# Joining float64 words into float32: three passes over 256 columns, or two over 512

## Chip, cores, metric

The kernel runs on one core of a Trainium2 chip. What counts is the device time of one execution in microseconds. The engines are named as the profile does: PE (TensorE), DVE (VectorE), ACT (ScalarE), POOL (GpSimd) and SP (SyncE, which issues most transfers); each works through its own queue in order.

## What is computed

```python
# q, k, v: (8, 8, 576, 64) float32; the five weights arrive as float64
attn = softmax(q @ mean_of_8(k).T / 8) @ mean_of_8(v)        # per head, 72 pooled keys
x = attn.transpose(0, 2, 1, 3).reshape(4608, 512)
h = x @ w_in                                                  # 512 x 2048
x = (h * clip(h + 3, 0, 6) / 6) @ w_out                       # 2048 x 512
g = x @ w_gate                                                # 512 x 1536
out = (g * sigmoid(g) * (x @ w_val)) @ w_out2                 # 1536 x 512
```

## The kernel before

TensorE multiplies in float32 pieces: each operand is kept as a high part and a low part (the rest), and each product is three matmuls, so that every weight and every activation is split once (`split`, lines 136 and 137: a cast on ScalarE gives the high part, a subtraction gives the low part).

The program has three stages. In the startup (to about 56 us) the attention of the first block of 512 tokens is computed. Then come nine token blocks (loop over j) of the first feed-forward part. A block has 16 iterations (f), one for each 128 columns of `w_in`: an up-projection into `h`, its activation (`act1`, lines 575 and 577), the split of the result `g` (`split_g`), and, two iterations later, the down-projection into `y` (`down1`); both products are on line 553. Between these, `attn_slot` puts the attention steps of the next block, in an order written out by hand. From about 1040 us on the second feed-forward part runs, as a Strassen-like scheme on prepared sums of weights.

The weights of the first part are needed from block 0 on, so they are converted during the startup and block 0. A float64 word arrives as two 32-bit words. `fetch` (line 104) loads them into a ring of staging tiles `wstg`, on SyncE's queue; `rescale` (line 115, ScalarE) multiplies the upper word, read as a float32, by 2^-112, which moves the exponent to its float32 place; `join` (VectorE) makes the float32 word in a tile `w` in three passes: line 120 shifts the upper word left by 4 and right by 1, line 126 ors in the lower word shifted right by 29, line 131 ors in the sign bit of the upper word. `split` then writes the parts into `wu` (up) or `fly` (down); the subtraction is on GpSimd. In block 0, and there alone, the split of `g` subtracts on GpSimd too; in the later blocks it does so on VectorE.

`Weights.convert` is one step of that pipeline: it splits what the call before joined, joins what the call before rescaled, rescales what has been fetched, and fetches anew. One call handles two pieces of 256 columns, that is one weight tile of 512 columns. The tiles `w` come from a pool of two buffers (`t_p`, tag w32), so one call uses both. There are 32 tiles, 16 up and 16 down, in the order up 0, up 1, down 0, up 2, down 1 and so on. In the startup some units call it once; in block 0 each iteration calls it twice. A finished down tile also goes to DRAM (`w1_d`), from where the later blocks read it.

The weights of the second part are prepared during blocks 1 to 7, in 18 units (`prep_step`), one every six iterations: four quarters of 256 columns are fetched, rescaled, and joined into the tile `q`; GpSimd forms sums of them, and the parts go to DRAM.

Of the kernel before, what the change touches and what calls it, by code (L numbers as in the profile page):

```python
# [8 lines left out]
F32 = mybir.dt.float32  # L9
# [14 lines left out]
def kernel(  # L24
# [54 lines left out]
    prep_ctx = ExitStack()  # L79
    stg_p = prep_ctx.enter_context(tc.tile_pool(name="stg", bufs=6, side="right"))  # L80
    q7_p = prep_ctx.enter_context(tc.tile_pool(name="q7", bufs=1, side="right"))
# [17 lines left out]
    wu = {}  # L99
    WC = 256  # L100

    def fetch(src):
        t = stg_p.tile([P, WC, 2], F32, tag="stg", name="wstg")
        nc.sync.dma_start(
            out=t.bitcast(I32).rearrange("p a b -> p (a b)") if len(src.shape) == 2
            else t.bitcast(I32).rearrange("p (k a) b -> p k (a b)", k=src.shape[1]),
            in_=src,
        )
        return t

    def rescale(stage):
        hi = stage[:, :, 1]
        nc.scalar.activation(out=hi, in_=hi, func=ACTF.Copy, scale=2.0 ** -112)

    def join(pieces):
        for stage, dst in pieces:
            hi = stage[:, :, 1].bitcast(I32)
            nc.vector.tensor_scalar(  # L120
                out=dst, in0=hi, scalar1=4, scalar2=1,
                op0=ALU.logical_shift_left, op1=ALU.logical_shift_right,
            )
# [15 lines left out]
    class Weights:  # L139


        def __init__(self):
            self.todo, self.staged, self.scaled, self.joined = [], [], [], []
            self.cur = {}

        def add_up(self, key, src, f):
            w = src.bitcast(I32).rearrange("(k p) f -> p k f", p=P)[:, :, 2 * P * f:2 * P * (f + 1)]
            for i in range(KT * P // WC):
                m = WC // P
                self.todo.append(("up", key, w[:, m * i:m * (i + 1)], i))  # L150

        def add_down(self, key, src, f):
            w = src.bitcast(I32)[f * P:(f + 1) * P, :]
            for i in range(DM // WC):
                self.todo.append(("down", key, w[:, 2 * WC * i:2 * WC * (i + 1)], i))

        def fetch(self):
            while self.todo and len(self.staged) + len(self.scaled) < 6:
                item = self.todo.pop(0)
                self.staged.append((item, fetch(item[2])))  # L160

        def convert(self, n=1):

            done, self.joined = self.joined, []
            for (kind, key, _, i), t in done:
                if i == 0:
                    if kind == "up":
                        self.cur[key] = wu_p.tile([P, 2, KT, P], F32R, tag="wu", name="wu")
                    else:
                        self.cur[key] = fly_p.tile([P, 2, DM], F32R, tag="fly", name="fly")  # L170
                w = self.cur[key]
                if kind == "up":
                    w = w.rearrange("p a k f -> p a (k f)")
                w = w[:, :, WC * i:WC * (i + 1)]
                split(w[:, 0], w[:, 1], f32(t), nc.gpsimd)
                if i == KT * P // WC - 1:
                    t = self.cur.pop(key)
                    (wu if kind == "up" else fly)[key] = t
                    if kind == "down":
                        nc.sync.dma_start(out=w1_d[key[1]], in_=f32(t))  # L180
# [42 lines left out]

    PREP = 6
    prep_t = {}

# [7 lines left out]
    def prep_step(u, step):  # L234
        kind, f, m = preps[u]
        if step == 0:
            place = A7 if kind == "up" else B7
            prep_t["q", u] = []
            for quarter in ("11", "12", "21", "22"):
                r, c = int(quarter[0]) - 1, int(quarter[1]) - 1  # L240
                if kind == "up":
                    w = (w_gate, w_val)[m].bitcast(I32).rearrange("(k p) f -> p k f", p=P)
                    src = w[:, 2 * c:2 * c + 2, 2 * P * (2 * f + r):2 * P * (2 * f + r + 1)]
                else:
                    w = w_out2.bitcast(I32)[P * (2 * f + r):P * (2 * f + r + 1), :]
                    src = w[:, 4 * P * c:4 * P * (c + 1)]
                prep_t["q", u].append((fetch(src), place[quarter]))
        elif step == 1:
            for s, _ in prep_t["q", u]:
                rescale(s)  # L250
        elif step == 2:
            q = prep_t["f", u] = q7_p.tile([P, 8, WC], F32, tag="q7", name="q7")
            join([(s, q[:, i].bitcast(I32)) for s, i in prep_t.pop(("q", u))])
        elif step == 3:
# [5 lines left out]
        elif step == 4:  # L260
            q, t = prep_t["f", u], s7_p.tile([P, 7, 2, WC], F32R, tag="s7", name="s7")
            prep_t["s", u] = t
# [643 lines left out]
    def do_step(st):  # L906
# [29 lines left out]
        elif what == "X":  # L936
            exps(units[i])
        elif what == "M":
            scale_e(units[i])
        elif what == "U":  # L940
            copy_a(units[i])
        elif what == "L":
            lo_a(units[i])
        elif what == "W":
            hi_x(units[i])
        elif what == "Y":
            lo_x(units[i])
# [16 lines left out]
    with tc.manual_schedule():  # L964
# [30 lines left out]
        while ("in", 1) not in wu:  # L995
            weights.convert(2)

# [23 lines left out]
        for n, (j, f) in enumerate(seq1):  # L1021
# [13 lines left out]
            g = act1(hp)  # L1035
            weights.convert(2 if j == 0 else 0)
            if n >= 2:
# [5 lines left out]
            split_g((1, j, f), g)  # L1043
            weights.convert(2 if j == 0 else 0)
            if j > 0:
# [76 lines left out]
```

## Time and profile before

| | us |
|---|---|
| median of 3 runs | 1835.23 (1834.75 to 1835.96) |
| the profiled execution | 1835.06 |
| its span, first to last instruction | 1833.3 |
| PE busy in the span | 1748.5 (95%) |
| DVE / ACT / POOL busy | 1258.8 / 686.8 / 676.6 |
| PE share of the chain that ended last | 81% |

Busy times are averages over stages with different limits. What a change in one stage is worth has to be read in that stage. Line numbers (L120) are those of the kernel before.

### The profile page before, as it was taken

The page shows a single profiled execution, that of the slowest core. Times are in us where ns is not written, and L with a number is a line of the kernel's source. Part 1 is how long each engine was busy: PE and PEld are TensorE (multiplying, and loading weights), DVE is VectorE, ACT ScalarE, POOL GpSimd, SP SyncE. Part 2 cuts the span into 40 slices and gives each one's busy share as a digit, 9 for nine tenths or more (in the row PEclk, how much of TensorE's full clock was granted, in tenths as well). Part 3 has the DMA queues.
Part 4 walks back from the last instruction along what each step waited for, and adds up shares of the span by engine and source line. Part 5 has one row for each costly group of instructions (what it writes and reads, how often), then busy time and mean ns, then how long its engine had stood idle before and what let it go on. Part 6 is the DMA issues. An engine that isn't in the chain of part 4 may idle for free.

```text
span 1833.3 us, 28479 instructions
## 1 busy us (share of the span) xinstructions
PE 1748.5 (95%) x9929; PEld 1575.9 (86%) x9929; DVE 1258.8 (69%) x2480; ACT 686.8 (37%) x1612; POOL 676.6 (37%) x833
## 2 busy tenths in 40 slices
PE   4687899999999998999999999999999999999999
PEld 3476688888878787878888899999999999999999
DVE  6787676876767677686542367767678668568666
ACT  5444344443444444444433223224224225124223
POOL 5455342331423325233114154153252352361450
PEclk8888999999999999999999999999999999999999
DMA  7555456665766656656553487887887977977876
GB/s 159 173 174 162 148 172 200 216 185 183 215 206 197 197 168 195 209 159 197 194 177 132 177 294 238 296 288 241 305 277 252 315 262 250 324 252 253 284 245 219
DMA packets 203103, 402.97 MB, mean 220 GB/s; under 512 B 90576, under 2 KB 126416, under 8 KB 192208
## 3 DMA queue, kind: packets, MB, share of 16 engines
q1 hardware_dynamic: 198256, 396.17, 66.9%
q10 hardware_dynamic: 4704, 4.98, 0.9%
q8 instruction: 79, 1.29, 0.3%
q14 instruction: 64, 0.52, 0.1%
HBM read 340.79 MB, written 60.29 MB: 219 GB/s over the span
## 4 chain that ended last, share of the span: by engine, by line
PE 81%; DVE 7%; DMA 5%; issue 2%; POOL 2%; ACT 2%; SPq 1%; ACTq 0%; POOLq 0%; DVEq 0%
PE b L660 43%; PE y L553 17%; PE h L553 16%; PE pss L445 2%; DMA y<-yo 1%; DVE w L126 1%; DVE w L131 1%; DMA vts<-in_v_dram 1%; PE pst L505 1%; DMA qs<-in_q_dram 1%; DVE w L120 1%; PE pst L509 1%; DVE kp L370 1%; DMA fly<-w1d 1%; PE psk L393 1%
## 5 line engine op out<-in xcount | busy, mean ns | idle before, releaser
L660 PE MATMUL b<-xc,wr 128*128 128x384 f32 x3024 | 525.2, 334 | 0.0
L660 PEld LDWEIGHTS b<-xc,wr 128*128 128x128 f32 x3024 | 524.0, 188 | 0.1
L553 PE MATMUL h<-x,wu 128*128 128x512 f32 x1728 | 435.3, 401 | 0.0
L553 PE MATMUL y<-g,fly 128*128 128x512 f32 x1728 | 430.2, 398 | 1.5 <-DMA fly<-w1d 0.8
L669 DVE TENSOR_TENSOR c<-c,b 128x384 f32<-128x384 f32 x504 | 265.2, 552 | 178.5 <-PE b L660 154.7
L553 PEld LDWEIGHTS h<-x,wu 128*128 128x128 f32 x1728 | 322.0, 191 | 65.3 <-DVE x L546 0.6
L553 PEld LDWEIGHTS y<-g,fly 128*128 128x128 f32 x1728 | 318.3, 189 | 66.4 <-ACT yo L594 1.0
L707 POOL TENSOR_TENSOR s<-s,c 128x384 f32<-128x384 f32 x144 | 142.4, 1013 | 400.2 <-ACT s L705 400.2
L660 PE MATMUL b<-wr,gc 128*128 128x256 f32 x2268 | 265.6, 279 | 0.0
L660 PEld LDWEIGHTS b<-wr,gc 128*128 128x128 f32 x2268 | 265.4, 188 | 0.0
L488 POOL TENSOR_TENSOR e<-e,sm 96x288 f32<-96x288 f32 (+3 forms) x85 | 73.5, 865 | 451.9 <-DVE sm L484 336.1
L714 POOL TENSOR_TENSOR gf<-s,c 128x384 f32<-128x384 f32 x144 | 168.2, 1192 | 67.3 <-DVE c L669 66.5
L136 ACT CAST gc<-gf 128x768 fp32r<-128x768 f32 x126 | 105.7, 839 | 186.6 <-POOL gf L714 101.0
L705 ACT ACTIVATE s<-c 128x384 f32<-128x384 f32 x144 | 73.5, 526 | 202.0 <-DVE c L669 200.9
L137 DVE TENSOR_TENSOR gc<-gf,gc 128x768 fp32r<-128x768 f32 x126 | 133.9, 1095 | 15.5 <-ACT gc L136 13.7
L137 DVE TENSOR_TENSOR g<-g,g 128x512 fp32r<-128x512 f32 x128 | 93.0, 727 | 67.1 <-ACT g L136 66.6
L577 DVE SCALAR_TENSOR_TENSOR g<-t,h 128x512 f32<-128x512 f32 x144 | 97.3, 676 | 59.9 <-ACT t L575 53.5
L136 ACT CAST g<-g 128x512 fp32r<-128x512 f32 x144 | 88.6, 615 | 85.5 <-PE y L553 46.0
L575 ACT ACTIVATE t<-h,three 128x512 f32<-128x512 f32 x144 | 98.2, 682 | 37.1 <-PE h L553 36.4
L475 ACT ACTIVATE e<-e 96x288 f32<-96x288 f32 (+3 forms) x85 | 35.3, 415 | 185.2 <-DVE e L472 183.9
L445 PE MATMUL pss<-kbd,qT 128*128 128x144 f32 (+2 forms) x336 | 63.2, 308 | 29.3 <-DVE x L546 26.4
L677 ACT COPY c<-b 128x384 f32<-128x384 f32 x72 | 33.9, 471 | 145.6 <-PE b L660 145.6
(106 smaller groups left out, 1723.0 us busy)
## 6 DMA issues: line engine op xcount, KB each, us to landing
wr<-sup SPq DMA_DIRECT2D x72, 1024.0 KB
fly<-w1d SPq DMA_DIRECT2D x128, 512.0 KB
wr<-sdn SPq DMA_DIRECT2D x84, 768.0 KB
wr<-sup SPq DMA_DIRECT2D x72, 768.0 KB
sup<-s SPq DMA_DIRECT2D x12, 1792.0 KB
wstg<-in_moe_w_out_dram SPq DMA_DIRECT2D x56, 256.0 KB
sdn<-s SPq DMA_DIRECT2D x6, 1792.0 KB
ystg<-y SPq DMA_DIRECT2D x24, 384.0 KB
```

The lines of the kernel that those rows point to most:

```text
L136: nc.scalar.copy(out=hi, in_=src)
L137: lo_engine.tensor_tensor(out=lo, in0=src, in1=f32(hi), op=ALU.subtract)
L445: nc.tensor.matmul(out=ps[:, i], lhsT=qT[:, i * qt:(i + 1) * qt], rhs=kbd_t[p], start=True, stop=True)
L488: nc.gpsimd.tensor_tensor(out=e3, in0=e3, in1=sm.to_broadcast(list(e3.shape)), op=ALU.mult)
L553: nc.tensor.matmul(out=ps, lhsT=w(kt, wh), rhs=x(kt, xh), start=first and n == 0, stop=last and n == 3 * len(kts) - 1,)
L575: nc.scalar.activation(out=t, in_=ps, func=ACTF.Relu, bias=three)
L577: nc.vector.scalar_tensor_tensor(out=g, in0=t, scalar=6.0, in1=ps, op0=ALU.min, op1=ALU.mult)
L660: nc.tensor.matmul(out=ps, lhsT=w(wh), rhs=x(xh), start=first and n == 0, stop=last and n == 2)
L669: add = lambda dst, a, b: nc.vector.tensor_tensor(out=dst, in0=a, in1=b, op=ALU.add)
L705: nc.scalar.activation(out=g[q], in_=c[q], func=ACTF.Sigmoid)
L707: nc.gpsimd.tensor_tensor(out=g[q], in0=g[q], in1=c[q], op=ALU.mult)
L714: nc.gpsimd.tensor_tensor(out=gf[p][:, GP[TURN[q]], f], in0=g[q], in1=c[q], op=ALU.mult)
```

## The change

Conversion pieces become 512 columns wide, and `join` has two passes in place of three.

- `rescale` uses ScalarE's Prelu with a scale of 2^-112 and a slope of 2^32 for negative values. A negative upper word gets an exponent larger by 32 than a positive one, so the bit that becomes the sign after a shift by 3 is set.
- `join` shifts the upper word left by 3, then ors in the lower word shifted right by 29.
- The ring of staging tiles holds three tiles of 512 columns in place of six of 256. `convert` handles one tile per call in place of two pieces; the calls stay where they were.
- In `prep_step` two quarters share one staging tile (two transfers into its halves), and one join writes both quarters of `q`.

```diff
-    stg_p = prep_ctx.enter_context(tc.tile_pool(name="stg", bufs=6, side="right"))
+    stg_p = prep_ctx.enter_context(tc.tile_pool(name="stg", bufs=3, side="right"))
...
-    WC = 256
+    WC = 512
...
-        nc.scalar.activation(out=hi, in_=hi, func=ACTF.Copy, scale=2.0 ** -112)
-
-    def join(pieces):
-        for stage, dst in pieces:
-            hi = stage[:, :, 1].bitcast(I32)
-            nc.vector.tensor_scalar(
-                out=dst, in0=hi, scalar1=4, scalar2=1,
-                op0=ALU.logical_shift_left, op1=ALU.logical_shift_right,
-            )
-        for stage, dst in pieces:
-            lo = stage[:, :, 0].bitcast(I32)
-            nc.vector.scalar_tensor_tensor(
-                out=dst, in0=lo, scalar=29, in1=dst, op0=ALU.logical_shift_right, op1=ALU.bitwise_or
-            )
-        for stage, dst in pieces:
-            hi = stage[:, :, 1].bitcast(I32)
-            nc.vector.scalar_tensor_tensor(
-                out=dst, in0=hi, scalar=-(2 ** 31), in1=dst, op0=ALU.bitwise_and, op1=ALU.bitwise_or
-            )
+        nc.scalar.activation(out=hi, in_=hi, func=ACTF.Prelu, scale=2.0 ** -112, alpha=2.0 ** 32)
+
+    def join(stage, dst, parts=1):
+        hi, lo = (stage[:, :, i].bitcast(I32) for i in (1, 0))
+        if parts > 1:
+            hi, lo = (t.rearrange("p (k n) -> p k n", k=parts) for t in (hi, lo))
+        nc.vector.tensor_scalar(
+            out=dst, in0=hi, scalar1=3, scalar2=None, op0=ALU.logical_shift_left,
+        )
+        nc.vector.scalar_tensor_tensor(
+            out=dst, in0=lo, scalar=29, in1=dst, op0=ALU.logical_shift_right, op1=ALU.bitwise_or
+        )
...
-            for i in range(KT * P // WC):
-                m = WC // P
-                self.todo.append(("up", key, w[:, m * i:m * (i + 1)], i))
+            self.todo.append(("up", key, w))
...
-            while self.todo and len(self.staged) + len(self.scaled) < 6:
+            while self.todo and len(self.staged) + len(self.scaled) < 3:
...
-            pieces = []
             scaled, self.scaled = self.scaled, []
             for item, s in scaled:
                 t = t_p.tile([P, WC], I32, tag="w32", name="w32")
-                pieces.append((s, t))
+                join(s, t)
                 self.joined.append((item, t))
-            join(pieces)
...
-            for quarter in ("11", "12", "21", "22"):
+            for pair in ((("11", "21"), ("12", "22")) if kind == "up" else (("11", "21"), ("22", "12"))):
+                t = stg_p.tile([P, WC, 2], F32, tag="stg", name="wstg")
+                for i, quarter in enumerate(pair):
...
+                    fetch_into(t[:, WH * i:WH * (i + 1)], src)
...
-            join([(s, q[:, i].bitcast(I32)) for s, i in prep_t.pop(("q", u))])
+            for s, at in prep_t.pop(("q", u)):
+                join(s, q[:, at].bitcast(I32), 2)
...
-            weights.convert(2)
+            weights.convert()
```

## Rows read from the trace of the kernel before

**Rows 1.** The page of the profile: span, and busy tenths of TensorE and VectorE and the granted TensorE clock in 40 equal slices of 45.8 us.

```profile
span 1833.3 us, 28479 instructions
...
PE   4687899999999998999999999999999999999999
...
DVE  6787676876767677686542367767678668568666
...
PEclk8888999999999999999999999999999999999999
```

**Rows 2.** The view by windows: start and end of a stretch in us, its length, busy us (and count) of PE, PEld, DVE, ACT and POOL, granted clock, DMA share, GB/s.

```profile
34.00:206.00 172.00, 125.97 (x590) 99.29 (x589) 135.36 (x339) 80.38 (x254) 91.33 (x130) 0.84 0.52 162
232.00:335.00 103.00, 102.71 (x520) 85.50 (x520) 77.88 (x185) 46.03 (x123) 33.27 (x54) 1.00 0.60 185
232.00:1040.00 808.00, 793.34 (x3858) 655.96 (x3858) 533.71 (x1189) 335.28 (x828) 248.04 (x360) 1.00 0.60 187
```

**Rows 3.** TensorE's timeline (start us, us, what): the first and the fourteenth up-projection of block 0, and a key pooling that ran without a stop; then, from the view of one source line, the first and last start of the 18 stores of finished blocks on ScalarE (line 594, two in each of 9 blocks).

```profile
56.41 5.37 PE L553 MATMUL h<-x,wu 128*128 128x512 f32 x12
...
121.67 2.02 PE L393 MATMUL psk<-ident,k_in 72*64 72x72 f32 x32
...
206.72 2.93 PE L553 MATMUL h<-x,wu 128*128 128x512 f32 x12
...
L594 ACT ACTIVATE yo<-y x18: 590/597/600, 222.7 to 1039.9; 128x512 f32<-128x512 f32 x18
```

**Rows 4.** The chain of waits between 34 and 206 us, shares by line (the view ends the line where it does), and what TensorE waited for longest in the same stretch (us in total, times, longest us).

```profile
by line: issue 14.3%; DVE w L126 10.3%; DVE w L131 8.6%; PE y L553 7.6%; PE h L553 7.0%; DVE w L120 6.3%; PE psk L393 5.4%; DMA wstg<-in_moe_w_in_dram 4.7%; POOL fly L137 4.2%; POOL wu L137 3.4%; PE pss L445 1.7%; ACT wu L136 1.7%; DVE x L5
...
PE pss L445 <- DVE x L546: 20.6, 6, 4.7
```

**Rows 5.** The view by windows for the instructions alone that write or read the tiles named w (the joined 32-bit words): busy us of DVE, ACT and POOL (and counts), then as in rows 2.

```profile
34.00:206.00 172.00, 89.62 (x192) 22.68 (x62) 44.75 (x62) 0.84 0.52 162
```

**Rows 6.** VectorE's groups between 34 and 206 us, by form: the shift of the conversion (busy us, mean ns | idle us of the engine before it, and what ended that).

```profile
L120 DVE TENSOR_SCALAR w<-wstg 128x256 int32<-128x256 int32 x64 | 35.1, 588 | 30.8 <-POOL wu L137 21.1 <-POOL fly L137 6.7 <-DMA q_in<-in_q_dram 2.8
```

**Rows 7.** The timeline (start us, us, engine, what): a conversion call that GpSimd did not disturb, and one pair that it did.

```profile
185.76 2.09 DVE L131 SCALAR_TENSOR_TENSOR w<-wstg,w 128x256 int32<-128x256 int32 x2
185.97 1.25 POOL L137 TENSOR_TENSOR g<-g,g 128x512 fp32r<-128x512 f32 x1
...
193.04 0.49 DVE L120 TENSOR_SCALAR w<-wstg 128x256 int32<-128x256 int32 x2
193.45 0.75 DVE L126 SCALAR_TENSOR_TENSOR w<-wstg,w 128x256 int32<-128x256 int32 x2
194.12 0.75 DVE L131 SCALAR_TENSOR_TENSOR w<-wstg,w 128x256 int32<-128x256 int32 x2
```

**Rows 8.** The view of source line 120: minimum, median and maximum ns, first and last start, in the later preparations (q) and in the conversion (w).

```profile
L120 DVE TENSOR_SCALAR q<-wstg x72: 279/285/836, 247.8 to 922.3; 128x256 int32<-128x256 int32 x72
L120 DVE TENSOR_SCALAR w<-wstg x64: 279/797/1371, 34.3 to 203.2; 128x256 int32<-128x256 int32 x64
```

**Rows 9.** SyncE's queue from 30 to 222 us: what the weight fetches (line 104) waited for longest (us in total, times, longest us); then two fetches in the timeline, and their landing as a piece of the chain of waits.

```profile
SPq L104 <- DVE w L131: 67.4, 28, 7.4
...
127.10 0.89 SPq L104 DMA_DIRECT2D wstg<-in_moe_w_in_dram  x2
...
127.58 2.75 DMA wstg<-in_moe_w_in_dram
```

**Rows 10.** VectorE's and GpSimd's groups between 34 and 206 us, by form: the product of the activation over 512 columns, and the subtractions of the conversion and of g.

```profile
L577 DVE SCALAR_TENSOR_TENSOR g<-t,h 128x512 f32<-128x512 f32 x14 | 9.4, 670 | 1.5 <-ACT t L575 1.4
...
L137 POOL TENSOR_TENSOR wu<-w,wu 128x256 fp32r<-128x256 f32 x32 | 23.2, 744 | 4.7 <-ACT wu L136 4.7
L137 POOL TENSOR_TENSOR fly<-w,fly 128x256 fp32r<-128x256 f32 x30 | 21.6, 740 | 13.3 <-ACT fly L136 13.3
L137 POOL TENSOR_TENSOR g<-g,g 128x512 fp32r<-128x512 f32 x14 | 18.9, 1353 | 2.3 <-ACT g L136 2.3
```

**Rows 11.** ScalarE's groups between 34 and 206 us, by form: the rescaling, a cast of the conversion and the cast of g.

```profile
L115 ACT ACTIVATE wstg<-wstg 128x256 f32<-128x256 f32 x61 | 23.3, 431 | 0.0
L136 ACT CAST fly<-w 128x256 fp32r<-128x256 f32 x30 | 10.8, 402 | 18.6 <-DVE w L131 6.6 <-issue 6.2 <-PE y L553 3.6
...
L136 ACT CAST g<-g 128x512 fp32r<-128x512 f32 x14 | 8.6, 614 | 0.1
```

**Rows 12.** The groups of the whole program by form: the table loads of ScalarE.

```profile
L968 ACT ACT_TABLE_LOAD x1 | 1.3, 1283 | 0.8 <-PEq L1107 0.8
L1051 ACT ACT_TABLE_LOAD x1 | 1.3, 1283 | 0.0
```

**Rows 13.** VectorE's timeline in block 1: the twelve operations of one later preparation.

```profile
247.78 0.89 DVE L120 TENSOR_SCALAR q<-wstg 128x256 int32<-128x256 int32 x4
248.59 1.42 DVE L126 SCALAR_TENSOR_TENSOR q<-wstg,q 128x256 int32<-128x256 int32 x4
249.93 1.42 DVE L131 SCALAR_TENSOR_TENSOR q<-wstg,q 128x256 int32<-128x256 int32 x4
```

More of the change, by code (lines that the diff above doesn't have):

```diff
@@ L99, with fetch_into @@
     wu = {}
-    WC = 256
+    WC = 512
     def fetch(src):
         t = stg_p.tile([P, WC, 2], F32, tag="stg", name="wstg")
+        fetch_into(t, src)
+        return t
+    def fetch_into(t, src):
         nc.sync.dma_start(
@@ L108, in fetch @@
         )
-        return t
     def rescale(stage):
         hi = stage[:, :, 1]
-        nc.scalar.activation(out=hi, in_=hi, func=ACTF.Copy, scale=2.0 ** -112)
-    def join(pieces):
-        for stage, dst in pieces:
-            hi = stage[:, :, 1].bitcast(I32)
-            nc.vector.tensor_scalar(
-                out=dst, in0=hi, scalar1=4, scalar2=1,
-                op0=ALU.logical_shift_left, op1=ALU.logical_shift_right,
-            )
-        for stage, dst in pieces:
-            lo = stage[:, :, 0].bitcast(I32)
-            nc.vector.scalar_tensor_tensor(
-                out=dst, in0=lo, scalar=29, in1=dst, op0=ALU.logical_shift_right, op1=ALU.bitwise_or
-            )
-        for stage, dst in pieces:
-            hi = stage[:, :, 1].bitcast(I32)
-            nc.vector.scalar_tensor_tensor(
-                out=dst, in0=hi, scalar=-(2 ** 31), in1=dst, op0=ALU.bitwise_and, op1=ALU.bitwise_or
-            )
+        nc.scalar.activation(out=hi, in_=hi, func=ACTF.Prelu, scale=2.0 ** -112, alpha=2.0 ** 32)
[9 more added lines that the diff above has]
+        )
     def split(hi, lo, src, lo_engine):
@@ L143, in __init__ @@
             self.todo, self.staged, self.scaled, self.joined = [], [], [], []
-            self.cur = {}
         def add_up(self, key, src, f):
             w = src.bitcast(I32).rearrange("(k p) f -> p k f", p=P)[:, :, 2 * P * f:2 * P * (f + 1)]
-            for i in range(KT * P // WC):
-                m = WC // P
-                self.todo.append(("up", key, w[:, m * i:m * (i + 1)], i))
+            self.todo.append(("up", key, w))
         def add_down(self, key, src, f):
-            w = src.bitcast(I32)[f * P:(f + 1) * P, :]
-            for i in range(DM // WC):
-                self.todo.append(("down", key, w[:, 2 * WC * i:2 * WC * (i + 1)], i))
+            self.todo.append(("down", key, src.bitcast(I32)[f * P:(f + 1) * P, :]))
         def fetch(self):
-            while self.todo and len(self.staged) + len(self.scaled) < 6:
+            while self.todo and len(self.staged) + len(self.scaled) < 3:
                 item = self.todo.pop(0)
@@ L164, in convert @@
             done, self.joined = self.joined, []
[L165 to L171, printed above, removed]
+            for (kind, key, _), t in done:
                 if kind == "up":
+                    w = wu[key] = wu_p.tile([P, 2, KT, P], F32R, tag="wu", name="wu")
                     w = w.rearrange("p a k f -> p a (k f)")
-                w = w[:, :, WC * i:WC * (i + 1)]
+                else:
+                    w = fly[key] = fly_p.tile([P, 2, DM], F32R, tag="fly", name="fly")
                 split(w[:, 0], w[:, 1], f32(t), nc.gpsimd)
[L176 to L180, printed above, removed]
-            pieces = []
+                if kind == "down":
+                    nc.sync.dma_start(out=w1_d[key[1]], in_=f32(w))
             scaled, self.scaled = self.scaled, []
@@ L224 @@
     PREP = 6
+    WH = WC // 2
     prep_t = {}
@@ L238, in prep_step @@
             prep_t["q", u] = []
-            for quarter in ("11", "12", "21", "22"):
[L240 to L247, printed above, removed]
+            for pair in ((("11", "21"), ("12", "22")) if kind == "up" else (("11", "21"), ("22", "12"))):
+                t = stg_p.tile([P, WC, 2], F32, tag="stg", name="wstg")
+                for i, quarter in enumerate(pair):
+                    r, c = int(quarter[0]) - 1, int(quarter[1]) - 1
+                    if kind == "up":
+                        w = (w_gate, w_val)[m].bitcast(I32).rearrange("(k p) f -> p k f", p=P)
+                        src = w[:, 2 * c:2 * c + 2, 2 * P * (2 * f + r):2 * P * (2 * f + r + 1)]
+                    else:
+                        w = w_out2.bitcast(I32)[P * (2 * f + r):P * (2 * f + r + 1), :]
+                        src = w[:, 4 * P * c:4 * P * (c + 1)]
+                    fetch_into(t[:, WH * i:WH * (i + 1)], src)
+                a, b = (place[quarter] for quarter in pair)
+                prep_t["q", u].append((t, slice(a, b + 1, b - a)))
         elif step == 1:
@@ L251, in prep_step @@
         elif step == 2:
-            q = prep_t["f", u] = q7_p.tile([P, 8, WC], F32, tag="q7", name="q7")
-            join([(s, q[:, i].bitcast(I32)) for s, i in prep_t.pop(("q", u))])
+            q = prep_t["f", u] = q7_p.tile([P, 8, WH], F32, tag="q7", name="q7")
+            for s, at in prep_t.pop(("q", u)):
+                join(s, q[:, at].bitcast(I32), 2)
         elif step == 3:
@@ L260, in prep_step @@
         elif step == 4:
-            q, t = prep_t["f", u], s7_p.tile([P, 7, 2, WC], F32R, tag="s7", name="s7")
+            q, t = prep_t["f", u], s7_p.tile([P, 7, 2, WH], F32R, tag="s7", name="s7")
             prep_t["s", u] = t
@@ L995 @@
         while ("in", 1) not in wu:
-            weights.convert(2)
+            weights.convert()
         def attn_slot(j, s):
@@ L1035 @@
             g = act1(hp)
-            weights.convert(2 if j == 0 else 0)
+            weights.convert(1 if j == 0 else 0)
             if n >= 2:
@@ L1043 @@
             split_g((1, j, f), g)
-            weights.convert(2 if j == 0 else 0)
+            weights.convert(1 if j == 0 else 0)
             if j > 0:
```

## The prediction

> **What bounds the kernel now.** I read the page's slices first. TensorE is near full from the seventh slice on; in the first five it is not, and its granted clock falls below full in slices two to five [rows 1]. A slice is 45.8 us, so whatever can be won lies in the first 220 us, where the weights are converted for the first time. The stage windows say the same [rows 2]: in the 808 us from 232 to 1040, the eight later token blocks, TensorE is busy 793 us at clock 1.00; between 34 and 206 us it is busy 126 of 172 us at clock 0.84. The weight conversion, all 32 tiles of it, runs just there.
>
> Next, the rows of TensorE. The first up-projection starts at 56.4 us, the fourteenth at 206.7 us: 13 iterations in 150 us, 11.6 us each [rows 3]. Later blocks take (1039.9 - 222.7)/8 = 102 us for 16 iterations, 6.4 us each [rows 3]. So block 0 pays about 5 us per iteration for something the later blocks don't have.
>
> What that is, the chain of waits tells: the three conversion operations of VectorE, lines 126, 131 and 120, hold 10.3 + 8.6 + 6.3 = 25% of it, and the GpSimd subtraction that follows them 7.6% [rows 4]. TensorE's own waits there end with VectorE results, x above all (20.6 us) [rows 4]. VectorE works on the w tiles for 89.6 of its 135.4 us [rows 2, 5], and stands idle another 30.8 us before line 120, of which 27.8 us end with GpSimd's subtraction on line 137 [rows 6]. That wait is a buffer wait: there are two w32 buffers, a call uses both, and the next call's shift may not overwrite them until GpSimd has read them. 135.4 + 30.8 = 166.2 of 172 us: VectorE, its buffer wait included, sets the stretch, with 3.5% left over (172/166.2 = 1.035).
>
> A second thing sits inside the 89.6 us. Undisturbed, a call's six operations run from 193.04 to 194.87 us, 1.83 us [rows 7]; 32 calls would be 58.6 us. The other 31 us are waits of started operations for GpSimd: the pair of line 131 at 185.76 took 2.09 instead of 0.75 us around a 1.25 us GpSimd subtraction [rows 7], and line 120 has a median of 797 ns here against 285 ns in the later stage [rows 8].
>
> **The change, part by part.**
> *Six VectorE operations of 256 columns become two of 512.* One shift and one shift-or per call are left. The pair of 256-column shifts took 0.49 us and one alone 0.28 us, so one shift over 512 lies between 0.28 and 0.49 us; I take 0.45, since it moves the pair's columns with one start fewer. The pair of shift-ors took 0.75 us, and the 512-column operation of the same kind on line 577 takes 0.67 [rows 7, 10]; I take 0.70. Together 1.15 us (0.95 to 1.24), 32 calls: 37 us, before waits for GpSimd.
>
> *The buffer wait goes.* A call now uses one of the two w32 buffers, so the next call's shift writes the other. 27.8 us of VectorE idling [rows 6] fall away. Behind the waiting shift stood everything else in VectorE's queue, x for TensorE's next scores among it, and the SyncE queue, which waited 67 us on line 131 before weight fetches, with the k, q and v loads behind them [rows 9].
>
> *GpSimd subtracts 512 columns at once.* The same operation on g costs 1.35 us over 512 columns, against 2 x 0.74 [rows 10]: 32 x 1.35 = 43 instead of 44.8 us.
>
> *ScalarE* rescales 512 columns with another function and casts 512. Before: 23.3 us of rescaling and 22.7 us of casts in the stretch [rows 5, 11]. The 512-column cast of g takes 0.615 us against 0.40 for 256 [rows 11]; the same step on 0.43 gives 0.645. 32 x 1.26 = 40 us, so ScalarE falls from 80.4 to 74.7 us of the stretch. It is not the bound; I count nothing. That covers the new function only if it needs no table load; the trace shows two loads in the whole program although Relu, Copy and Exp alternate [rows 12], but no Prelu.
>
> *Fetches.* A weight tile comes in one transfer instead of two, with the same bytes and the same lead of two calls. Two fetches issued at 127.10 us had landed at 130.33, 3.2 us later [rows 9]; at two calls per iteration of some 8 us the lead is about 8 us. Nothing, as long as a call takes over 1.6 us.
>
> *The 18 later preparations* lose 8 of 12 VectorE operations. Undisturbed, a unit's twelve ran from 247.78 to 251.35 us, 3.6 us; 2 x 1.15 = 2.3 us remain. The 1.3 x 18 = 23 us lie under a TensorE that is busy 793 of 808 us [rows 2, 13]. I count nothing; if a part of it shows, it can be at most those 15 us.
>
> *The sum for 34 to 206 us.* VectorE: 45.7 us of other work + 37 = 82.5 us, plus 64 operations times a wait w for GpSimd. The trace has no such row for 1.35 us operations; w lies between 0 and one whole subtraction, 1.35. I take half of one, 0.67, since neither engine now waits for the other's buffer and they meet at any phase: 82.5 + 43 = 126 us. A second count comes to the same: if GpSimd's operations and these VectorE operations never overlap, as the stretched pair in rows 7 suggests, the two need 46.6 + 43 + 37 = 127 us one after the other. TensorE needs less: 22.4 us until the first up-projection, 13 x 6.4 = 83, and three key poolings of 2.0 us [rows 3], 111 us. I take 127 us with the 3.5% of before, 131 us: 41 us saved. The profiled execution took 1835.06 us (span 1833.3; the median of the runs is 1835.23), so 1835 - 41 = **1794 us**.
>
> *What the skill says of w.* The Trainium skill, "SBUF — State Buffer", section "Who interferes with whom", has VectorE and GpSimd share a pair of SBUF ports as an exclusive lock: a shift in its two-port mode, or any operation with two SBUF inputs, blocks for the whole of a GpSimd operation already running, and the other way round. The 2.09 us pair agrees. It speaks against this change, since longer operations hold the lock longer; without the lock the sum would be TensorE's 111 us, with it 127 us.
>
> **Rivals.**
> *B: TensorE becomes the bound.* Waits fall where nothing hangs on them. 111 x 1.035 = 115 us, 57 us saved: 1778 us. For it: the later blocks hold TensorE at 99% with VectorE at 75% [rows 2]. Against: GpSimd is busy a third there, and would be at 90 of 131 us here.
>
> *C: waits for GpSimd eat the gain.* VectorE's shifts meet GpSimd's 1.35 us subtractions again and again. At w = 1.0 the stretch takes (82.5 + 64) x 1.035 = 152 us, 1815 us; at a whole subtraction each, 175 us, 1838 us. From w = 1.31 it is slower than before. For it: the waits in rows 7 and 8. Against: before, 31 us over 192 operations were 0.16 us each.
>
> *D: the other side, table loads.* If Prelu is not in the table that holds Exp, each call needs two loads of 1.28 us [rows 12], 82 us over 32 calls. Filling ScalarE's idle time they make (74.7 + 82) x 1.035 = 162 us, 1825 us; put end to end with the chain, 131 + 82 = 213 us, 1876 us. In the middle 1850 us, slower. ScalarE alone would set a slower stretch from 1.43 us a load. Against: Relu and Copy already cost no load beside Exp. The Trainium skill, "ScalarE: Activation LUTs", section "Table sets: the hidden batching unit", says that cheap functions are in every set, but doesn't name Prelu among them; its section on the load's cost puts a switch at 2.66 us with the drain, which would make it 245 us and some 1917 us in all. The trace has no drain beside its 1.28 us.
>
> *E: nothing moves.* The conversion shortens, but TensorE's waits in block 0 pass to attention's chain. 1835 us. Against it stand the 25% of the chain.
>
> **How the numbers follow.** My forecast A 0.56 (1784 to 1803 us), B 0.14, C 0.20, D 0.04, E 0.06. A change of 0.2% (3.7 us) is about the least that a measurement of this kernel tells from none. A, B and three quarters of C are faster: 0.85. E and a tenth of C are the same: 0.08. D and the rest of C are slower: 0.07. The range runs from 1775 us (B, and 3 us of the later preparations) to 1818 us (C up to about w = 1.05); outside lie D, E, the dear end of C and a little of B, 0.2 together.
>
> **What would show it.** Right: the shift idles no more before GpSimd's line 137; 32 shifts of 512 columns at 0.45 us plus a wait near half a subtraction; VectorE near 125 us busy or less up to the last conversion, which ends near 165 us; the fourteenth up-projection near 165 us; clock 1.0 in more of the first five slices; still two table loads; the span from 232 us on, shifted, unchanged. Wrong: mean shift or shift-or over 1.6 us (C), over two loads (D), TensorE above 97% from its first up-projection (B), waits of TensorE on GpSimd or ScalarE in place of VectorE (E).

## The result: 1786 us, and where the 49 us came from

The changed kernel takes 1786.1 us (median, 1785.96 to 1788.77) against 1835.6 us: ratio 0.9732, 95% interval 0.9716 to 0.9749. The forecast was 1794 us, range 1775 to 1818. Its sign and its main mechanism held. The saving is 8 us larger than forecast, and of the steps of the prediction that were wrong only one moved the time: the later preparations, by about those 8 us.

The page of the changed kernel's profile, lines as in [rows 1]. Its slices are 44.6 us long.

```profile
span 1784.2 us, 28034 instructions
...
PE   4889999999999999999999999999999999999999
...
DVE  7897677768567666765522468568668568668666
...
PEclk9899999999999999999999999999999999999999
```

TensorE is at nine tenths from the fourth slice on, where it was from the sixth [rows 1], and its granted clock is at nine tenths or more in all slices but the second. VectorE's third slice is at nine tenths: it is no less full than before, for a shorter time.

From TensorE's timeline, the first up-projection of block 0 and the one that stood at 206.72 us [rows 3]:

```profile
50.47 5.07 PE L543 MATMUL h<-x,wu 128*128 128x512 f32 x12
...
166.99 2.93 PE L543 MATMUL h<-x,wu 128*128 128x512 f32 x12
```

39.7 us are saved up to there, against 41 forecast; 5.9 of them lie before the first up-projection, which stood at 56.41 us, and 33.8 in block 0. (The up-projection at 206.72 us, which rows 3 and the prediction call the fourteenth, is the sixteenth and last of block 0.) The views by windows of that stretch, all instructions and then those of the tiles w alone (columns as in [rows 2] and [rows 5]):

```profile
34.00:167.00 133.00, 115.22 (x596) 91.19 (x594) 120.38 (x212) 75.06 (x195) 93.10 (x99) 0.92 0.69 208
```

```profile
34.00:167.00 133.00, 72.12 (x63) 19.70 (x32) 41.21 (x31) 0.92 0.69 208
```

The stretch has 133 us where it had 172 and where 131 were forecast. TensorE's own work in it fell from 126.0 to 115.2 us, at a granted clock of 0.92 in place of 0.84. VectorE's groups in it, by form (busy us, mean ns | idle before):

```profile
L129 DVE SCALAR_TENSOR_TENSOR w<-wstg,w 128x512 int32<-128x512 int32 x32 | 49.5, 1546 | 1.1
L126 DVE TENSOR_SCALAR w<-wstg 128x512 int32<-128x512 int32 x31 | 22.9, 737 | 3.9 <-POOL wu L135 3.9
```

The idle time before the shift has gone from 30.8 us [rows 6] to 3.9. The conversion itself went only from 89.6 to 72.1 us, although a third of its passes is gone: the shift-or takes 1546 ns on the mean. The view of source lines 126 and 129 has what they take at best (minimum, median, maximum ns):

```profile
L126 DVE TENSOR_SCALAR w<-wstg x32: 399/428/2116, 33.3 to 164.0; 128x512 int32<-128x512 int32 x32
...
L129 DVE SCALAR_TENSOR_TENSOR w<-wstg,w x32: 691/1109/3539, 33.8 to 164.5; 128x512 int32<-128x512 int32 x32
```

The rest is waiting for GpSimd. The longest of these operations in the timeline (start us, us):

```profile
125.32 0.41 DVE L126 TENSOR_SCALAR w<-wstg 128x512 int32<-128x512 int32 x1
125.55 0.71 POOL L478 TENSOR_TENSOR e<-e,sm 96x288 f32<-96x288 f32 x1 [0.83 <-ACT wu L134]
125.77 3.54 DVE L129 SCALAR_TENSOR_TENSOR w<-wstg,w 128x512 int32<-128x512 int32 x1
126.22 1.29 POOL L135 TENSOR_TENSOR g<-g,g 128x512 fp32r<-128x512 f32 x1
127.47 1.28 POOL L135 TENSOR_TENSOR wu<-w,wu 128x512 fp32r<-128x512 f32 x1
```

The shift-or was to start at 125.77, inside a GpSimd operation. It waited not for that one alone but for the next two as well, which followed without a gap, and ended 0.56 us after the third, at 129.31.

ScalarE's rescaling (128 x 512, whole program) and its table loads:

```profile
L120 ACT ACTIVATE wstg<-wstg 128x512 f32<-128x512 f32 x68 | 43.9, 673 | 0.6 <-DMA wstg<-in_moe_w_out_dram 0.6
L958 ACT ACT_TABLE_LOAD x1 | 1.3, 1283 | 0.8 <-PEq L1097 0.8
L1041 ACT ACT_TABLE_LOAD x1 | 1.3, 1283 | 0.0
```

Prelu brought no table load.

The other 9 us lie where nothing was counted. Views by windows of blocks 1 to 7, from block 1's first up-projection to block 8's, in the kernel before and in the changed one:

```profile
212.20:947.90 735.70, 720.27 (x3541) 594.93 (x3540) 519.43 (x1175) 311.68 (x801) 230.11 (x352) 1.00 0.61 189
```

```profile
172.50:898.90 726.40, 718.79 (x3542) 596.01 (x3541) 492.37 (x1031) 309.76 (x765) 225.45 (x352) 1.00 0.61 191
```

TensorE's work is the same (720 and 719 us); its gaps, the stretch less its busy time, fell from 15.4 to 7.6 us, and VectorE's busy time by 27 us. From block 8 on both kernels take the same: 1833.3 - 947.9 = 885.4 us and 1784.2 - 898.9 = 885.3 us.

### The profile page after: what moved, and what is told of

It reads as the page before. It is cut to its first block, busy times and chain, and to the rows that moved or that the text cites. A ratio compares the mean times of both kernels' runs of the same rounds, so it can differ in the third digit from the quotient of the medians.

```text
span 1784.2 us, 28034 instructions
## 1 busy us (share of the span) xinstructions
PE 1736.6 (97%) x9929; PEld 1569.3 (88%) x9929; DVE 1217.2 (68%) x2208; ACT 678.9 (38%) x1512; POOL 673.7 (38%) x801
## 4 chain that ended last, share of the span: by engine, by line
PE 88%; DVE 4%; DMA 3%; issue 2%; POOL 1%; ACT 1%; SPq 0%; ACTq 0%; DVEq 0%; POOLq 0%
PE b L650 44%; PE y L543 19%; PE h L543 19%; PE pss L435 2%; DVE w L126 1%; PE pst L495 1%; DVE w L129 1%; DMA y<-yo 1%; PE pst L499 1%; DMA q_in<-in_q_dram 1%; DMA qs<-in_q_dram 1%; DMA fly<-w1d 1%; PE psv L524 1%; PE psv L522 0%; PE psv L523 0%
## 5 line engine op out<-in xcount | busy, mean ns | idle before, releaser
L199 DVE TENSOR_TENSOR gf<-gf 128x768 f32<-128x768 f32 (+1 forms) x66 | 66.9, 1029 | 12.1 <-POOL gf L704 10.9
```

What stands on the lines that cost most here:

```text
L199: eng.tensor_tensor(out=v(what), in0=v(a), in1=v(b), op=op)
```

## Experiments

All runs in one table. The starts and lengths of blocks are from TensorE's timeline of each profile, from first up-projection to first up-projection. "Conversion" is VectorE's time in the passes over w plus its idle time before the shift, from the groups by form; the passes overlap a little, so that the sum of their times, 94.6 us in the kernel before, stands above the 89.6 us of rows 5. "16th" is the start of block 0's last up-projection.

| kernel | median us | conversion us | 16th at us | block 0 us | blocks 1 to 7 us |
|---|---|---|---|---|---|
| before | 1835.6 | 94.6 + 30.8 | 206.7 | 155.8 | 735.7 |
| e1: before, four w32 buffers | 1826.9 | 116.5 + 0.1 | 197.7 | 148.9 | 738.6 |
| e4: before, two passes | 1808.8 | 63.8 + 34.0 | 188.9 | 141.3 | 726.4 |
| e8: before, two passes and four buffers | 1793.4 | 79.5 + 0.1 | 172.3 | 126.6 | 728.4 |
| e3: changed, three passes | 1818.0 | 98.9 + 0.7 | 191.5 | 142.7 | 731.6 |
| e2: changed, one w32 buffer | 1813.8 | 44.4 + 53.6 | 191.8 | 143.9 | 727.2 |
| e9: changed, old preparations | 1792.5 | 72.6 + 3.9 | 167.7 | 122.1 | 736.4 |
| changed | 1786.1 | 72.4 + 3.9 | 167.0 | 122.0 | 726.4 |
| e11: changed again | 1785.7 | 69.2 + 3.7 | 166.5 | 120.0 | 728.5 |
| e5: changed, GpSimd writes zeros | 1775.3 | 49.7 + 0.1 | 155.4 | 112.2 | 728.1 |
| e7, e12: changed, g on VectorE | 1783.0, 1783.6 | 66.3 + 0 | 162.3, 162.9 | 116.2, 117.6 | 726.6, 726.8 |
| e6: changed, weights on VectorE | 1789.3 | 47.9 + 0 | 169.6 | 124.6 | 728.5 |
| e10: changed, g and down on VectorE | 1786.2 | 55.1 + 0 | 166.5 | 121.4 | 725.3 |

(The expectations count up-projections as the prediction did; their "fourteenth" is this sixteenth.)

**Which part of the change carries what.** Theory: VectorE, its buffer wait included, sets block 0, and passes and buffer share the gain. Four runs undo or do one part.

*e1: the buffer alone.*

```diff
-                t = t_p.tile([P, WC], I32, tag="w32", name="w32")
+                t = t_p.tile([P, WC], I32, tag="w32", name="w32", bufs=4)
```

> The kernel before with four w32 buffers in place of two: three passes over 256 columns as before, but the next call's shift no longer writes a buffer that GpSimd still reads. Theory (VectorE sets the stretch, its buffer wait included): the 27.8 us of idling before the shift fall away, VectorE's own work stays at about 135 us plus somewhat more waiting for GpSimd inside started operations, so 15 to 30 us are saved: 1805 to 1820 us. Rival 1 (the wait was only the outside of the shared-port wait, and moves into the operations): under 6 us saved, 1829 to 1836 us. Rival 2 (the buffer wait is the whole of the gain): over 42 us saved, under 1793 us.

Measured: 1826.9 us, ratio 0.9953 (0.9937 to 0.9968): 9 us, under the theory's 15 to 30 and over the rival's 6. VectorE's groups show why (34 us to the sixteenth up-projection):

```profile
L126 DVE SCALAR_TENSOR_TENSOR w<-wstg,w 128x256 int32<-128x256 int32 x64 | 46.4, 764 | 0.0
L131 DVE SCALAR_TENSOR_TENSOR w<-wstg,w 128x256 int32<-128x256 int32 x64 | 37.6, 626 | 0.0
L120 DVE TENSOR_SCALAR w<-wstg 128x256 int32<-128x256 int32 x63 | 32.5, 555 | 0.1
```

The 30.8 us of idling are gone to 0.1, but the three passes grew from 94.6 to 116.5 us. Of the wait 22 us came back as longer operations, 9 stayed saved, and 9 is what the time shows. So the first rival was nearer the mark than the theory: on this reading, waiting for the buffer had also kept the operations out of GpSimd's way.

*e4: the passes alone* (Prelu and the two-pass join put into the kernel before, pieces of 256 columns).

```diff
-        nc.scalar.activation(out=hi, in_=hi, func=ACTF.Copy, scale=2.0 ** -112)
+        nc.scalar.activation(out=hi, in_=hi, func=ACTF.Prelu, scale=2.0 ** -112, alpha=2.0 ** 32)
...
-                out=dst, in0=hi, scalar1=4, scalar2=1,
-                op0=ALU.logical_shift_left, op1=ALU.logical_shift_right,
+                out=dst, in0=hi, scalar1=3, scalar2=None, op0=ALU.logical_shift_left,
...
-        for stage, dst in pieces:
-            hi = stage[:, :, 1].bitcast(I32)
-            nc.vector.scalar_tensor_tensor(
-                out=dst, in0=hi, scalar=-(2 ** 31), in1=dst, op0=ALU.bitwise_and, op1=ALU.bitwise_or
-            )
```

> The kernel before with Prelu and two passes, over pieces of 256 columns and with two buffers as before: the new sign without width and without the free buffer. Theory: line 131 held 30.6 us of VectorE, its pair 0.75 us undisturbed; 24 to 31 us are saved: 1804 to 1812 us. Rival (the buffer wait grows by what the pass gives back, because the shift waits for GpSimd anyway): under 10 us saved, over 1825 us. In both cases two table loads and a rescaling of 430 ns.

Measured: 1808.8 us (0.9860, 0.9842 to 0.9878), 27 us, in the theory's range. 18 us lie before the sixteenth up-projection, 9 in blocks 1 to 7. The buffer wait did not take the pass's place (34.0 us against 30.8):

```profile
L120 DVE TENSOR_SCALAR w<-wstg 128x256 int32<-128x256 int32 x64 | 34.9, 584 | 34.0 <-POOL wu L131 23.5 <-POOL fly L131 8.6 <-DMA wstg<-in_moe_w_in_dram 1.7
```

*e3: width and buffer without the third pass's removal.*

```diff
-        nc.scalar.activation(out=hi, in_=hi, func=ACTF.Prelu, scale=2.0 ** -112, alpha=2.0 ** 32)
+        nc.scalar.activation(out=hi, in_=hi, func=ACTF.Copy, scale=2.0 ** -112)
...
-            out=dst, in0=hi, scalar1=3, scalar2=None, op0=ALU.logical_shift_left,
+            out=dst, in0=hi, scalar1=4, scalar2=1,
+            op0=ALU.logical_shift_left, op1=ALU.logical_shift_right,
...
+        nc.vector.scalar_tensor_tensor(
+            out=dst, in0=hi, scalar=-(2 ** 31), in1=dst, op0=ALU.bitwise_and, op1=ALU.bitwise_or
+        )
```

> The changed kernel with the three passes and the Copy rescaling of before, over 512 columns: the width and the free buffer without the new sign. Theory: one more shift-or per call, 0.70 us undisturbed and some 1.5 with its wait for GpSimd, 22 to 48 us more VectorE work in a stretch that VectorE nearly fills: 1806 to 1830 us. Rival (width and buffer carry the gain, the third pass hides under TensorE): within 8 us of the changed kernel, 1786 to 1794 us.

Measured: 1818.0 us (0.9902, 0.9887 to 0.9916), 32 us slower than the changed kernel, as the theory had it. This run also prices Prelu: its Copy over the same 512 columns takes 672 ns on the mean, Prelu 673.

*e2: the passes and the width without the free buffer.*

```diff
-                t = t_p.tile([P, WC], I32, tag="w32", name="w32")
+                t = t_p.tile([P, WC], I32, tag="w32", name="w32", bufs=1)
```

> The changed kernel with one w32 buffer of 512 columns: two wide passes, but the buffer wait is back, and a whole 1.33 us subtraction long. Theory: VectorE is 91% busy up to the fourteenth up-projection, so a wait of 0.6 to 1.3 us per call shows nearly in full, less what it saves in waits inside the operations: 15 to 35 us slower than the changed kernel, 1801 to 1821 us. Rival (the buffer wait only stands in place of the shared-port wait): within 6 us of it, 1784 to 1792 us.

Measured: 1813.8 us (0.9884, 0.9866 to 0.9901), 28 us slower than the changed kernel, in the theory's range. The shift's group:

```profile
L126 DVE TENSOR_SCALAR w<-wstg 128x512 int32<-128x512 int32 x32 | 18.8, 587 | 53.6 <-POOL wu L135 32.1 <-POOL fly L135 21.4
```

53.6 us of idling came back, and the operations themselves fell to 44.4 us. The 28 us are the price of one buffer of 512 columns; they can't be set beside the 9 us of e1, which had two buffers of 256 to start from. At that width the free buffers are worth 9 us with three passes (e1) and 15 with two (e4 against e8, below).

*e8: all but the width*, the kernel of e4 with four buffers.

```diff
-                t = t_p.tile([P, WC], I32, tag="w32", name="w32")
+                t = t_p.tile([P, WC], I32, tag="w32", name="w32", bufs=4)
```

> The kernel before with Prelu, two passes and four w32 buffers, over pieces of 256 columns: all of the change but the width. Undisturbed a call costs VectorE 0.49 + 0.75 = 1.24 us against 0.42 + 0.69 = 1.11 over 512 columns, 4 us over 32 calls. Theory (passes and buffer carry the gain): 1784 to 1794 us. Rival (width carries its own part, by halving the number of operations that can meet GpSimd): 1796 to 1809 us, near the kernel with two passes and two buffers.

Measured: 1793.4 us (0.9770, 0.9755 to 0.9784): at the dear end of the theory. VectorE's groups:

```profile
L125 DVE SCALAR_TENSOR_TENSOR w<-wstg,w 128x256 int32<-128x256 int32 x64 | 50.4, 825 | 0.0
L120 DVE TENSOR_SCALAR w<-wstg 128x256 int32<-128x256 int32 x64 | 29.1, 494 | 0.1
```

The width is worth 7 us, not 4: the 128 operations of 256 columns take 79.5 us, the 64 wide ones 69 to 72. Passes and buffers together carry 43 of the 49 us; singly they bring 27 (e4) and 9 (e1), 36 in all, so the parts don't quite add.

**What the conversion waits for.** Theory: VectorE's started operations wait for GpSimd operations that read SBUF. To see it, GpSimd was left as busy as before but without those reads.

*e5: zeros in place of the low parts*, which this kernel leaves out of the first weights.

```diff
-                split(w[:, 0], w[:, 1], f32(t), nc.gpsimd)
+                nc.scalar.copy(out=w[:, 0], in_=f32(t))
+                for _ in range(3):
+                    nc.gpsimd.memset(f32(w[:, 1]), 0.0)
```

> The changed kernel, but the low parts of the first feed-forward part's weights are left out: GpSimd writes zeros three times over the 512 columns (some 1.4 us, as long as the subtraction) instead of subtracting, so that in the conversion it reads nothing from SBUF. Theory (VectorE's started operations wait for GpSimd operations that read): shift-or falls from 1.55 us to 0.7 to 1.1 (the split of g and attention still read), block 0 from 122.0 to 106 to 116 us, 1770 to 1780 us in all. Rival (GpSimd's own occupation, or TensorE and the attention chain, set block 0): shift-or falls too, but block 0 stays within 3 us of 122, 1783 to 1789 us. Second rival (the shift-or is long for another reason, its wide operands or the transfers into SBUF): shift-or stays above 1.4 us.

Measured: 1775.3 us (0.9664, 0.9647 to 0.9680), block 0 112.2 us. VectorE's groups, and the two blocks 0 by windows, of the changed kernel and of this one:

```profile
L129 DVE SCALAR_TENSOR_TENSOR w<-wstg,w 128x512 int32<-128x512 int32 x32 | 31.3, 977 | 1.1
L126 DVE TENSOR_SCALAR w<-wstg 128x512 int32<-128x512 int32 x32 | 18.4, 576 | 0.1
```

```profile
50.50:172.50 122.00, 110.09 (x579) 88.64 (x579) 107.92 (x175) 66.08 (x159) 87.89 (x90) 0.97 0.67 209
```

```profile
48.70:160.90 112.20, 106.74 (x579) 87.51 (x578) 87.67 (x177) 66.33 (x159) 92.22 (x148) 0.98 0.79 233
```

GpSimd is busy for 92 us in 112, more than the 88 in 122 before it, and still block 0 is 10 us shorter and VectorE 20 us less busy. So GpSimd's occupation is not what set it. The timeline of this run has both cases:

```profile
83.96 1.27 POOL L166 MEMSET wu<- 128x512 f32 x2
84.81 0.69 DVE L129 SCALAR_TENSOR_TENSOR w<-wstg,w 128x512 int32<-128x512 int32 x1
85.18 1.11 POOL L166 MEMSET fly<- 128x512 f32 x2
...
97.33 0.69 POOL L480 TENSOR_TENSOR e<-e,sm 96x288 f32<-96x288 f32 x1 [0.38 <-DVE sm L476]
97.53 2.29 DVE L129 SCALAR_TENSOR_TENSOR w<-wstg,w 128x512 int32<-128x512 int32 x1
97.98 1.29 POOL L135 TENSOR_TENSOR g<-g,g 128x512 fp32r<-128x512 f32 x1
99.21 1.12 POOL L166 MEMSET wu<- 128x512 f32 x2
```

Amid zero writes the shift-or takes its 0.69 us. Amid two GpSimd operations that read, it takes 2.29 us and ends 0.55 us after the second, while zero writes already run again. So it goes with all 32: the twelve that met zero writes alone took 0.69 us each, the 19 that met an operation that reads took 0.80 to 2.29 (one met nothing, 0.69). The times of the whole run would leave a doubt, since the zeros also spare GpSimd the wait for ScalarE's cast; the single operations do not. The Trainium skill, "SBUF — State Buffer", section "Who interferes with whom", says that an operation of VectorE with two SBUF inputs contends with a GpSimd instruction that reads SBUF and not with one that only writes it; this run agrees.

*e7 and e12: g on VectorE.* Block 0's split of g subtracts on VectorE, as in the later blocks.

```diff
-        split(gt[:, 0], gt[:, 1], g, nc.gpsimd if key[:2] == (1, 0) else nc.vector)
+        split(gt[:, 0], gt[:, 1], g, nc.vector)
```

> The changed kernel with block 0's split of g subtracting on VectorE, as the later blocks do: GpSimd loses 16 operations of 1.45 us, VectorE gains 16 of about 0.73 us plus their waits. Theory (the two engines take turns on what both read): the sum of the two falls by 16 x 0.7 = 11 us, but VectorE, 91% busy, gets 12 us more and loses perhaps as much in waits: block 0 between 116 and 124 us, 1780 to 1788 us. Rival (GpSimd's occupation is the bound): block 0 falls by 15 us or more, under 1772 us. Rival (VectorE's work alone is the bound): block 0 grows by 8 us or more, over 1793 us.

> The changed kernel with block 0's split of g on VectorE, again, with more rounds. Theory (taking turns on what both read costs more than VectorE's 12 us of added work): 2 to 5 us faster than the changed kernel beside it. Rival (the 3 us of the first look are scatter): within 1.5 us of it.

Measured: 1783.0 us (0.9711, 0.9697 to 0.9725), then 1783.6 us (0.9707, 0.9693 to 0.9721) beside 1785.7 us (0.9719, 0.9704 to 0.9734) for e11, the changed kernel again on the same chip:

> The changed kernel again, to stand on the same chip beside the three that follow: 1784 to 1788 us.

Neither engine alone is the bound: VectorE's 12 us of added work are paid by fewer waits (it is busy 107 us of block 0 with them, 107 to 108 without), and block 0 is 2 to 6 us shorter. Both times the kernel is 2 to 3 us faster, but the intervals overlap, so a version that beats the changed kernel is likely and not shown.

*e6 and e10: the weights' subtraction on VectorE*, for all tiles, and for the down tiles with g.

```diff
-                split(w[:, 0], w[:, 1], f32(t), nc.gpsimd)
+                split(w[:, 0], w[:, 1], f32(t), nc.vector)
```

For e10, with the edit of e7:

```diff
-                split(w[:, 0], w[:, 1], f32(t), nc.gpsimd)
+                split(w[:, 0], w[:, 1], f32(t), nc.gpsimd if kind == "up" else nc.vector)
```

> The changed kernel with the weights' subtraction in the conversion on VectorE, the split of g on GpSimd: VectorE gains 32 operations of 0.73 us, 23 us, and its 64 conversion operations no longer meet GpSimd's subtraction of weights, about 0.7 us a call less, 22 us. Theory: even on VectorE, block 0 between 118 and 126 us, 1782 to 1790 us. Rival (VectorE's waits are nearly all from this subtraction): block 0 near the 112 us of the run without its reads plus some of the 23 us, under 1780 us. Rival (VectorE's own work decides): block 0 over 130 us, over 1794 us.

> The changed kernel with the split of g and the subtraction of the 16 down tiles on VectorE, that of the 16 up tiles on GpSimd. Theory: against the kernel with g alone moved, VectorE gains 16 x 0.73 = 12 us and loses about as much in waits: 1780 to 1786 us, no clear gain over it. Rival (VectorE is full): 1788 us or more.

Measured: 1789.3 us (0.9739, 0.9724 to 0.9754) and 1786.2 us (0.9724, 0.9709 to 0.9739), the first in its theory's range, the second at the upper edge. In e6 the conversion falls to 47.9 us, as low as with zeros, but the 32 subtractions cost VectorE 25.7 us: what the waits give back the work takes. Moving work between the two engines gains little here; only taking it away does (e5).

**The later preparations.**

*e9: the changed conversion, the old preparations*; `rescale_copy` and `join3` are the rescaling and the three passes of the kernel before.

```diff
             for s, _ in prep_t["q", u]:
-                rescale(s)
+                rescale_copy(s)
...
+            pieces = []
             for s, at in prep_t.pop(("q", u)):
-                join(s, q[:, at].bitcast(I32), 2)
+                for i, n in enumerate((at.start, at.start + at.step)):
+                    hi, lo = (s[:, WH * i:WH * (i + 1), c].bitcast(I32) for c in (1, 0))
+                    pieces.append((hi, lo, q[:, n].bitcast(I32)))
+            join3(pieces)
```

> The changed kernel with the 18 later preparations as before: Copy, and three passes over four quarters of 256 columns, twelve VectorE operations a unit. Theory (the 9 us that blocks 1 to 7 became shorter come from the preparations' shorter VectorE stretch): blocks 1 to 7 return from 726 to 733 to 738 us, 1792 to 1798 us in all, block 0 unchanged at 122. Rival (they come from elsewhere, a shifted phase or the state of the transfers): within 3 us of the changed kernel, 1783 to 1789 us.

Measured: 1792.5 us (0.9767, 0.9752 to 0.9782), and blocks 1 to 7 by windows:

```profile
173.20:909.60 736.40, 723.36 (x3542) 596.95 (x3541) 518.75 (x1175) 308.60 (x765) 228.18 (x352) 1.00 0.60 189
```

736.4 us, as in the kernel before, and block 0 unchanged at 122.1. So the 9 us belong to the preparations. How many they are is less sure: this profiled execution was the slowest of its kernel's four (1796.7 us, the others 1791.2 to 1792.6), and by the medians the old preparations cost 6 to 7 us. The profiles of all runs bear out the order: blocks 1 to 7 take 736 to 739 us with the old preparations (before, e1, e9), 731.6 with three passes over 512 columns (e3), and 725 to 729 with two passes. e4, with two passes over 256 columns, has 726.4: it is the third pass, and the width adds nothing that shows.

What TensorE waited for longest in blocks 1 to 7 (us in total, times, longest us), in the changed kernel and in the one before:

```profile
PE psv L524 <- DVE vtl L414: 2.8, 1, 2.8
PE pss L435 <- DVE x L536: 1.8, 2, 1.2
```

```profile
PE pss L445 <- DVE x L546: 5.7, 6, 2.1
PE psv L534 <- DVE vtl L424: 4.3, 3, 2.5
```

Half of the waits for x stand behind the joins in VectorE's queue. In the kernel before, these three, 2.6 us together, ended 0.2 to 0.4 us after the last pass of a preparation (which ended at 370.50, 732.32 and 771.97 us):

```profile
370.75 0.73 PE L445 MATMUL pss<-kbd,qT 128*96 128x144 f32 x4 [0.87 <-DVE x L546]
...
732.57 0.73 PE L445 MATMUL pss<-kbd,qT 128*96 128x144 f32 x4 [1.17 <-DVE x L546]
...
772.36 0.73 PE L445 MATMUL pss<-kbd,qT 128*96 128x144 f32 x4 [0.53 <-DVE x L546]
```

In the changed kernel none does. The longest waits for vtl are of another kind: 2.5 us at 717.67 us before and 2.8 us at 669.97 us in the changed kernel, both after GpSimd had sat idle over 7 us for a transfer of v, with no join near. By which waits the rest of the 9 us came through is not shown.

## Why the prediction held, and where not

**The stretch is VectorE's, its buffer wait included: held.** Over e1 to e4, e8 and the changed kernel, the conversion with its idle time went from 125 to 76 us and the sixteenth up-projection from 206.7 to 167.0, in the same order but for a microsecond or two. From there on less comes through: the 26 us that e5 takes off bring 12, since TensorE then is busy 107 of block 0's 112 us.

**The size of the stretch, 131 us: held, at 133, in part by luck.** The terms: the shift, taken at 0.45, has a median of 0.43; the shift-or, taken at 0.70, a minimum of 0.69; undisturbed a call runs 1.06 us (208.45 to 209.51 us in a later unit) against 1.15. The wait, taken at 0.67 an operation, came to (72.1 - 32 x 1.06)/64 = 0.60. But it is not half of one subtraction for either: the shift-or waits about 0.85, the shift about 0.3, and a started operation does not wait only for the GpSimd operation already running, as the prediction had it, but for up to three in a row. That the mean came near 0.67 is luck. VectorE's busy time came out at 120.4 us, 6 under the sum's 126; in return it idled 3.9 us before the shift, counted at nothing, and nearly 9 us are left over where 4 were taken. Rival C (w of 1.0 and over) did not come, though single waits went past its dearest case.

**The buffer wait: right in sign, wrong in worth by itself.** It was taken as 27.8 us that fall away. e1 shows that in the kernel before 22 of 31 us would have come back inside the operations, and 9 stayed; with two passes it is worth 15 us (e4 against e8). The forecast came out right because its sum charged w anew to all 64 operations.

**TensorE's floor, and with it rival B: wrong.** The up-projection at 206.72 us is the sixteenth of block 0, not the fourteenth; TensorE's timeline has sixteen starts from 56.41 to 206.72. So there are 15 iterations, of 10.0 us, and by the prediction's own terms the floor is 22.4 + 15 x 6.4 + 6 = 124 us, not 111. With 3.5% that is 129 us, 1792 us: so counted, B was no cheaper case below the forecast, it was nearly the forecast. Its first term was no floor either: in the changed kernel the first up-projection came 16.5 us into the stretch, not 22.4, and in e5 the sixteenth came after 121.4. B itself did not come: TensorE was busy 110 of block 0's 122 us, 90%, where B's sign was over 97%. The count did not enter the sum, as VectorE's terms did not use it; it made the low end of the range lower than these terms give.

**The later preparations, counted at nothing: wrong.** The step said that 23 us of VectorE lie under a TensorE busy 793 of 808 us, and left at most 15 us open. VectorE's time in blocks 1 to 7 fell by 27 us, and 9.3 us came through in the two profiles, 6 to 7 by e9's median. What failed is taking a busy share for a cover: 7.8 of TensorE's 15.4 us of gaps went with the shorter preparations, and 2.6 us of those gaps stood directly behind a join. With 39.7 us from the stretch the 9.3 make the 49 us.

**The reading of the slices: off by one.** Rows 1 show TensorE at nine tenths from the sixth slice on, and the clock below nine tenths in slices one to four. The sum does not use it. The conclusion drawn there, that whatever can be won lies in the first 220 us, failed by the same 9 us.

**ScalarE and the table loads: right.** 0.645 us were taken for the rescaling, 0.678 measured in the stretch; two loads, rival D did not come. The Trainium skill, "ScalarE: Activation LUTs", section "Table sets: the hidden batching unit", names tanh, relu and abs among the functions that come with exp, in a list that it breaks off, and not Prelu. Here Prelu ran beside Exp, Relu and Copy without a load of its own, at Copy's price (673 against 672 ns).

**Fetches, GpSimd's subtraction: right.** The subtraction takes 1.33 us; ScalarE waited for a fetch 0.6 us in all.

## What to carry to other kernels

A wait for a buffer and a wait for a shared resource can stand in for each other: take one away alone and the other grows, so price them together, with the resource's wait charged anew to each operation that is left. An engine that is 98% busy need not hide what another engine does beside it: look at who ends its few waits, and whether the edit shortens what stands ahead of them. Before a count of iterations carries a floor, count the starts in the timeline.

## What the runs showed of the hardware

A shift-or of VectorE that meets GpSimd reads need not be served after the running operation: in the changed kernel, at 125.77 us, it waited for three in a row, 3.54 us for 0.69 us of work; at 73.39 us it was served after the one that ran, 1.67 us, though the next followed without a gap. Zero writes by GpSimd don't hold it up: 0.69 us in all twelve such cases of e5. Over 512 columns with a stride of two words, undisturbed, the shift takes 0.42 us and the shift-or 0.69, over 256 columns (e4) 0.28 and 0.41: per added column the shift costs half as much.

Open is what block 0 still has over block 1 once most of the waits are gone: in e5 112.2 against 104.2 us, of which three key poolings of 2.0 us, which only block 0 has TensorE do, explain 6.
